# Moving state sums, spread decays, weight loads and weight sums in a fused state-space scan and routed expert layer

## The chip, the cores and the metric

The kernel runs on one core of a Trainium2 chip. Its time is the device time of one execution in microseconds; before the change it was 281.32 us (median of 3 runs, 279.15 to 281.43). The profile is one more execution, recorded on its own: its span, from the first to the last instruction, is 264.6 us. In what follows PE is the matrix engine, DVE the vector engine, ACT the scalar engine, POOL the GpSimd engine and SP the engine that only starts transfers.

## What is computed

The first half is a scan over a state. Batch 4, 8 heads, 768 steps, head size 32, state size 16. Per head, with `a` the decay of each step:

```python
log_a = np.log(np.clip(a, 1e-06, 1.0))
for c in range(nc):                       # chunks of the sequence
    cum = np.cumsum(la, axis=-1)
    L = np.exp(cum[:, :, :, None] - cum[:, :, None, :]) * causal
    M = np.einsum('bhin,bhjn->bhij', Cc, Bc) * L
    y_intra = np.einsum('bhij,bhjd->bhid', M, xc)
    y_inter = np.einsum('bhin,bhnd->bhid', Cc, state) * np.exp(cum)[:, :, :, None]
    y[:, :, sl] = y_intra + y_inter
    state = decay_full[:, :, None, None] * state + np.sum(Bx, axis=2)
```

The second half takes the 3072 tokens of the result, each 256 wide (8 heads of 32), and sends each to one of 8 experts: the one whose embedding has the largest cosine with it. The expert computes `relu(x @ w1[e]) @ w2[e]` with 1024 hidden units, and the result is multiplied by the token's softmax probability for that expert (temperature 0.1), the gate.

## The kernel before

**The scan** works on chunks of 128 steps (6 of them) and on pairs of batches: 12 pairs `p`, two to a chunk. In place of the exponentials of differences it scales: F holds running products of the decays and r their inverses; C is multiplied by F and x by r (x'), and only the causal mask is then left to apply. The steps of one pair, each a function of that name:

- `spread_f` (PE, L278): copies F of the pair's heads over the 16 state rows of each, into PSUM. `scale_c` (DVE, then ACT, L289): C times that, the tile `cp`, and from it two masked copies, `cm`.
- `scale_x` (DVE or POOL, L260): x' for the pair.
- `sums` (PE, L300): B times x' for each batch of the pair. After the second pair of a chunk `states` (DVE, L313) adds them to the decayed old state, the tile `V`, and `next_states` (POOL, L324) decays it into `old`.
- `inner` (PE, L333): B times C for the 8 heads of both batches, into the four PSUM banks of `pg`. `keep_inner` (DVE, L348): that times the mask, two instructions, the tiles `g`.
- `outputs_before` and `outputs_within` (PE, L365 and L381): the part of y from the old state and the part from within the chunk, both summed in PSUM, half of the heads in `pf` and half in `py`. `keep_outputs` (ACT, L396) copies both halves to `yT`.
- `finish` (PE, L412): turns `yT` back to one token to a partition, and computes the 8 routing scores by the same product, into `pz`. `keep_tokens` (ACT, L423) copies this to `yt`.

The main loop of `mamba` (L491) is a software pipeline written out by hand. In its turn `i` it makes F, `cp` and `sums` of pair `i + 2`, `inner` and `g` of pair `i`, outputs of pair `i - 1` and tokens of pair `i - 2`. Below it also routes: `pick` (DVE, even turns) finds each token's expert, `locate` (PE, then DVE, odd turns) its row in that expert's list, and `scatter` (POOL) writes the rows to memory, one transfer for each batch. When four chunks are scattered, the first 208 rows of expert 0 are loaded back as the tile `xe`, and the kernel starts on them (`early`) after the last pair.

The order in this text is the order on every engine: within `manual_schedule` nothing is reordered, and each engine takes its instructions one after the other. Waits between engines are set automatically. In PSUM they are set by whole banks, so that two engines that touch different columns of one bank are put in the order of the text all the same.

**PSUM in the scan** has eight banks: four for `pg`, one for `py`, one for `pf`, two for `pz`. Before the change, `sums` lie in the first 256 columns of `pf` (of `py` for the first chunk), the outputs in the first 256 of `py` and the last 256 of `pf`, the turned outputs in the first 264 of each bank of `pz`, and the spread F beside them, in columns 264 to 391. `locate`, `count` and the turned inverse decays use what is left of `py`.

**The weights** are 2 MB for an expert. `weights` (L239) cuts them in eight transfers of 256 KB: four for `w1` (64 partitions each, rows of 4 KB) and four for `w2` (128 partitions, rows of 1 KB). The loop starts one such transfer a turn from turn 4, three from turn 8; SP waits for nothing in between, so the profile shows 13 of them between 31.7 and 47.2 us.

**The experts.** A job is a set of rows of one expert: `parts[0]` and `parts[1]` are early and late rows of expert 0 (plain products, class `Job`), `parts[2]` and those after it are the whole experts 1 to 7 (class `Seven`, which replaces eight block products by seven and needs sums of weight blocks for it). `mix_up` and `mix_down` (L912, L916) compute these sums on POOL, m1 from `w1` and m2 from `w2`, four instructions each (L909). `mix_x` (DVE, L921) computes differences of the rows, the tile `dx`; `mix_h` (DVE, L989) those of the hidden units. `measure` and `prepare` (L778, L803) compute the gates. `part(i)` (L1072) runs one job; after its gates POOL executes a small copy, the tick (L1123), and then the sums of the job after next. Before the change, m2 of `parts[2]` is computed in the middle of `part(1)`, after the fourth of its eight `up` steps.

Of the kernel before, what the change touches and what calls it, by code (L numbers as in the profile page):

```python
# [226 lines left out]
    k.ld[c] = t  # L227


def load_w1(k, t, w1):  # L230
# [8 lines left out]
def weights(k, e):  # L239

    k.w1t[e] = k.wp.tile([128, KD, F], F32, name="w1", tag="w1")
    yield from load_w1(k, k.w1t[e], k.w1[e])
    k.w2t[e] = k.wp.tile([128, KF, DM], F32, name="w2", tag="w2")
    w2 = k.w2[e].rearrange("(f p) m -> p f m", p=128)
    for f in range(0, KF, 2):
        k.nc.sync.dma_start(k.w2t[e][:, f : f + 2, :], w2[:, f : f + 2, :])
        yield


def load_weights(k, e):  # L250
    for _ in weights(k, e):
        pass


def pair(k, p):
# [16 lines left out]

def forms(k, p):

    return k.pf[:, 0:256].rearrange("p (i m) -> p i m", i=2) if p in (1, 3) else k.pz[:, :, 264:392]


def spread_f(k, p):  # L278
# [21 lines left out]
def sums(k, p):  # L300

    c, b, t = pair(k, p)
    for i in range(2):
        for q in range(4):
            k.nc.tensor.matmul(
                (k.pf if c else k.py)[32 * q : 32 * q + 32, 64 * (b + i) : 64 * (b + i) + 64],
                lhsT=t.b[:, b + i, 32 * q : 32 * q + 32],
                rhs=k.un[p].x[:, i, :].rearrange("p (t q d) -> p q t d", t=2, q=4)[:, q],
                start=True, stop=True, tile_position=(0, 32 * q),
            )  # L310


def states(k, c):  # L313

    nc = k.nc
    st = (k.pf if c else k.py)[:, 0:256].rearrange("p (b m) -> p b m", b=NB)
    V = k.V[c] = k.stp.tile([128, NB, 64], F32, name="V", tag="V")
    if c == 0:
        nc.vector.tensor_copy(out=V[:], in_=st)
        return  # L320
    nc.vector.tensor_tensor(out=V[:], in0=k.old[c - 1][:], in1=st, op=ALU.add)


def next_states(k, c):  # L324
# [71 lines left out]
def keep_outputs(k, p):  # L396
    s = k.un[p]
    s.yT = k.yT[p] = k.work.tile([128, 2, 2, Q], F32, name="yT", tag="yT", bufs=3)
    if p == NU // 2 - 1:
        k.nc.scalar.copy(out=s.yT[:].rearrange("p j i m -> p j (i m)"), in_=k.pg[:, 0:2, 0:256])  # L400
        return
    for j in (1, 0):
        k.nc.scalar.copy(
            out=s.yT[:, j].rearrange("p i m -> p (i m)"), in_=k.pf[:, 256:512] if j == 0 else k.py[:, 0:256]
        )


# [22 lines left out]
def mamba(k):  # L430
# [49 lines left out]
    join(k, 0, k.pz[:, 1, 448:480])  # L480
    keep_inner(k, 1, 1)
    next_states(k, 0)
    outputs_within(k, 0)
    turn_emb(k)
    keep_outputs(k, 0)
    states(k, 1)
    scale_x(k, 4)
    route_consts(k)
    first = (None for e in range(2) for _ in weights(k, e))

    for i in range(2, NP):  # L491
        new = i + 2 if i + 2 < NP else None
# [24 lines left out]
        if pick_now == EC - 1:  # L517
            locate(k, pick_now)
            count_early(k)
        for j in range(2):  # L520
            keep_inner(k, i, j)
        if i < 6:
            next(k.dec[1])
        if pick_now == EC - 1:
            split_early(k)
            scatter(k, pick_now, 0, NB, None)
            load_early(k)
        if i % 2 == 0 and i // 2 < NC - 1:
# [529 lines left out]
def moe(k):  # L1058
# [13 lines left out]
    def part(i):  # L1072
# [14 lines left out]
        if isinstance(j, Seven):  # L1087
            portions = j.measures()
            for f in range(KF // 2):
                if i == EE + 1:  # L1090
                    j.up(f)
                    out(f)
                else:
                    j.up(f, lambda: (out(f), new or next(portions)))
                if not new and f == KF // 2 - 1:

                    k.nc.gpsimd.drain()  # L1097
            j.up(KF // 2, new.turn_x if new else None)
            if not new:
                j.mix_h((1, 0))  # L1100
                j.down_last(lambda: j.prepare(has))
                return
            j.mix_h()
            turn()
            j.down(lambda: j.prepare(has), (lambda: leftover(k)) if i == n - 3 else None)
        else:
            for f in range(KF):
                j.up(f)
                out(f - 1)
                if f == 3:  # L1110
# [214 lines left out]
```

## Time and profile before

| what | value |
|---|---|
| time, median of 3 | 281.32 us |
| span of the profiled execution | 264.6 us |
| scan, from the first `inner` to the last `finish` | 8.3 to 75.9 us |
| load of `xe` started, first use of it | 72.9, 76.2 us |
| first instruction of the first whole expert on PE | 103.2 us |
| time of one turn of the loop (turns 2 to 9, start to start on PE) | 4.5, 4.6, 4.8, 6.0, 8.5, 5.9, 4.5, 5.2 us |
| one `keep_inner` pair, one `scale_c`, one `scale_x` on DVE | 2.35, 0.41, 0.68 us |
| one weight sum on POOL | 1.27 us |

The page lists for each engine its busy time, then 40 equal slices of the span with the busy share of each engine in tenths, the clock that PE was granted in tenths and the share of the DMA engines. A list of waits names who waited for whom, the total, how often, and the longest. A timeline gives start and busy time of each instruction, with the idle time before it and what ended it in brackets.

### The profile page before, as it was taken

The numbers are of one execution on the slowest core, as the hardware profiler recorded it, in microseconds if no ns is written. First come the engines' busy times: TensorE is split into PE (matmuls) and PEld (weight loads), VectorE is DVE, ScalarE is ACT, GpSimd is POOL, SyncE is SP. The second block draws the span as 40 slices with busy tenths as digits, with TensorE's granted clock in tenths as the row PEclk, the third lists the DMA queues.
The fourth block names the chain that finished last, engine by engine and source line by source line (L and its number), as shares of the span: only waits on it lengthen the run. The fifth ranks groups of instructions, "written<-read, shape, count | busy, mean of one in ns | idle before, by whom it ended". The sixth has DMA issues, their size and how long they took to land. (4 is left out here: it accounts for less than half of the span.)

```text
span 264.6 us, 5990 instructions
## 1 busy us (share of the span) xinstructions
PE 244.8 (93%) x2133; PEld 223.4 (84%) x2133; DVE 186.1 (70%) x537; ACT 100.7 (38%) x313; POOL 167.8 (63%) x237
## 2 busy tenths in 40 slices
PE   2999987898989997999999999999999999999990
PEld 1887766776779797899999999999999999999980
DVE  6767897388838449668659668758867866975950
ACT  2335433343344240352445344353355234426310
POOL 4437227275658297992897698498499679635114
PEclk9999999799999999999999999999999999999998
DMA  5989999931262799706708526543570120102002
GB/s 173 385 347 325 383 264 228 233 118 66 108 217 108 164 251 216 210 14 178 221 8 211 176 56 161 150 135 114 120 217 19 44 73 0 55 2 64 0 0 64
DMA packets 19748, 38.89 MB, mean 147 GB/s; under 512 B 2893, under 2 KB 11290, under 8 KB 19717
## 3 DMA queue, kind: packets, MB, share of 16 engines
q1 hardware_dynamic: 16853, 31.94, 43.2%
q0 software_dynamic: 2688, 6.50, 7.8%
q8 instruction: 17, 0.28, 0.5%
q14 instruction: 14, 0.11, 0.2%
q10 hardware_dynamic: 176, 0.06, 0.1%
HBM read 28.37 MB, written 10.37 MB: 146 GB/s over the span
## 5 line engine op out<-in xcount | busy, mean ns | idle before, releaser
L888 POOL DMA_INDIRECT out_dram<-yo,to x32 | 39.5, 1235 | 19.0 <-DVE yo L884 6.3
L932 PE MATMUL sum<-dx,m 128*128 128x208 f32 x168 | 41.1, 349 | 1.8 <-ACT yoT L872 1.5
L940 DVE TENSOR_TENSOR part<-sum,part 128x208 f32<-128x208 f32 x69 | 25.5, 370 | 24.3 <-ACT part L945 17.9
L688 POOL DMA_INDIRECT rows<-yt,row_of x24 | 23.7, 988 | 21.9 <-DVE row_of L677 8.3
L909 POOL TENSOR_TENSOR m<-w 128x512 f32<-128x512 f32 x28 | 35.8, 1278 | 0.2
L940 DVE TENSOR_TENSOR h<-sum,part 128x208 f32<-128x208 f32 x84 | 29.2, 369 | 8.2 <-PE sum L932 5.2
L932 PEld LDWEIGHTS sum<-dx,m 128*128 128x128 f32 x168 | 29.0, 190 | 5.3 <-DVE part L940 3.3
L932 PE MATMUL sum<-dh,m 128*128 128x208 f32 x168 | 30.8, 339 | 0.0
L351 DVE TENSOR_TENSOR g<-pg,mask 128x1024 f32<-128x1024 f32 x24 | 28.3, 1216 | 2.4 <-PE pg L342 2.4
L932 PEld LDWEIGHTS sum<-dh,m 128*128 128x128 f32 x168 | 29.7, 190 | 0.0
L932 PE MATMUL sum<-xT,w 128*128 128x208 f32 x112 | 25.6, 339 | 0.0
L945 ACT COPY part<-sum 128x208 f32<-128x208 f32 x42 | 13.9, 331 | 25.6 <-PE sum L932 25.6
L932 PE MATMUL sum<-h,w 128*128 128x208 f32 x112 | 20.8, 339 | 0.0
L932 PEld LDWEIGHTS sum<-xT,w 128*128 128x128 f32 x112 | 20.1, 190 | 0.0
L985 ACT ACTIVATE h<-h 128x208 f32<-128x208 f32 x28 | 10.6, 377 | 25.1 <-DVE h L940 25.1
L932 PEld LDWEIGHTS sum<-h,w 128*128 128x128 f32 x112 | 19.8, 190 | 0.0
L342 PE MATMUL pg<-cm,bt 32*128 32x256 f32 x192 | 18.4, 463 | 0.8 <-DVE g L351 0.7
L909 POOL TENSOR_TENSOR m<-m,w 128x512 f32<-128x512 f32 x14 | 17.9, 1275 | 1.1
L909 POOL TENSOR_TENSOR m<-w,m 128x512 f32<-128x512 f32 x14 | 18.0, 1284 | 0.0
L800 POOL TENSOR_TENSOR gr<-gr,half 104x4 f32<-104x4 f32 (+1 forms) x9 | 9.2, 1021 | 13.3 <-ACT sq L794 13.3
L976 ACT ACTIVATE h<-h 128x208 f32<-128x208 f32 x28 | 10.6, 377 | 14.2 <-DVE h L940 14.2
L297 ACT ACTIVATE cm<-cp,tmask 128x256 f32<-128x256 f32 x24 | 10.8, 500 | 12.5 <-DVE cp L294 10.6
(234 smaller groups left out, 516.0 us busy)
## 6 DMA issues: line engine op xcount, KB each, us to landing
w<-in_moe_w_dram SPq DMA_DIRECT2D x64, 256.0 KB
rows<-none SPq DMA_DIRECT2D x8, 442.0 KB
xg<-rows SPq DMA_DIRECT2D x7, 442.0 KB
x<-in_x_dram SPq DMA_DIRECT2D x6, 512.0 KB
ct<-in_CT_dram SPq DMA_DIRECT2D x6, 256.0 KB
bt<-in_BT_dram SPq DMA_DIRECT2D x6, 256.0 KB
b<-in_B_dram SPq DMA_DIRECT2D x6, 256.0 KB
out_dram<-yo,to POOLq DMA_INDIRECT x32, 2.6
```

Source lines behind the costliest of these rows:

```text
L297: k.nc.scalar.activation(s.cm[:, :, v, :], s.cp[:], ACT.Copy, scale=k.tmask[:, v : v + 1])
L342: nc.tensor.matmul(k.pg[:, q, 256 * i : 256 * i + 256], lhsT=t.bt[r, b + i, :], rhs=s.cm[r, i], start=True, stop=True, tile_position=(32 * ...
L351: k.nc.vector.tensor_tensor(out=g[:], in0=k.pg[:, :, 256 * i : 256 * i + 256].rearrange("p q (t i) -> p q t i", t=2), in1=k.mask[:].unsque ...
L688: d = nc.gpsimd.indirect_dma_start(out=k.rows[:, :], out_offset=bass.IndirectOffsetOnAxis(ap=k.to[g][:, u : u + 1], axis=0), in_=k.yt[:, N ...
L800: nc.gpsimd.tensor_tensor(out=s.r[:], in0=s.r[:], in1=k.half[0:tr, 0:nt], op=ALU.pow)
L888: d = nc.gpsimd.indirect_dma_start(out=k.out[:, :], out_offset=bass.IndirectOffsetOnAxis(ap=s.to[:, i : i + 1], axis=0), in_=y[:], in_offs ...
L909: s.k.nc.gpsimd.tensor_tensor(out=out, in0=in0, in1=in1, op=op)
L932: s.k.nc.tensor.matmul(ps, lhsT=lhsT(i, g), rhs=rhs(j, g), start=(first and g == gs[0]), stop=(g == gs[-1]), skip_group_check=True,)
L940: s.k.nc.vector.tensor_tensor(out=out, in0=in0, in1=in1, op=ALU.add)
L945: s.k.nc.scalar.copy(out=out, in_=ps)
L976: nc.scalar.activation(o[:, 3], o[:, 3], ACT.Relu)
L985: nc.scalar.activation(o[:, 2], o[:, 2], ACT.Relu)
```

## The change

Four things are moved; what is computed stays the same.

1. `sums` go to columns 264 to 391 of `pz`, beside the turned outputs. They are now issued ahead of `finish`, and `states` follows directly after `keep_tokens`, where it stood after `keep_outputs`. The purpose is that `V` no longer shares a bank with the outputs.
2. The spread F goes to the last 256 columns of `pf`, where `sums` and the second half of the bank made room (in the start-up, for p = 1 to `pz` and for p = 3 to `py`). Both output halves now lie in the first 256 columns. `inner` is issued ahead of `spread_f`. `between` of the start-up moves from `pz` to `py`, and `turn_decays` of the second half of the decays from the middle of turn 5 to its end.
3. The first weights are loaded in the order w2 of expert 0, w1 of expert 0, w1 of expert 1, w2 of expert 1.
4. m2 of the first whole expert is computed after the tick of `part(1)`.

```diff
-    return k.pf[:, 0:256].rearrange("p (i m) -> p i m", i=2) if p in (1, 3) else k.pz[:, :, 264:392]
+    if p == 1:
+        return k.pz[:, :, 264:392]
+    return (k.py[:, 0:256] if p == 3 else k.pf[:, 256:512]).rearrange("p (i m) -> p i m", i=2)
...
-                (k.pf if c else k.py)[32 * q : 32 * q + 32, 64 * (b + i) : 64 * (b + i) + 64],
+                k.pz[32 * q : 32 * q + 32, b // 2, 264 + 64 * i : 328 + 64 * i],
...
-    st = (k.pf if c else k.py)[:, 0:256].rearrange("p (b m) -> p b m", b=NB)
+    st = k.pz[:, :, 264:392]
...
-    return k.pf[:, 256 + 128 * i : 384 + 128 * i] if j == 0 else k.py[:, 128 * i : 128 * i + 128]
+    return (k.py if j else k.pf)[:, 128 * i : 128 * i + 128]
...
-    between(k, 0, k.pz[:, 1, 448:480])
+    between(k, 0, k.py[:, 256:288])
...
     next_states(k, 0)
+    states(k, 1)
     outputs_within(k, 0)
     turn_emb(k)
     keep_outputs(k, 0)
-    states(k, 1)
...
-    first = (None for e in range(2) for _ in weights(k, e))
+    first = (
+        None for p in (w2_portions(k, 0), w1_portions(k, 0), w1_portions(k, 1), w2_portions(k, 1)) for _ in p
+    )
...
+        inner(k, i)
         if new is not None:
             spread_f(k, new)
             scale_c(k, new)
-        inner(k, i)
         if place_now is not None:
             locate(k, place_now)
-        if i == 5:
-            turn_decays(k, 1, k.py[:, 384:512])
...
+        if new is not None and c < NC - 1:
+            sums(k, new)
         finish(k, done)
         keep_tokens(k, done)
+        if new is not None and i % 2 and c < NC - 1:
+            states(k, c)
...
-        if new is not None and c < NC - 1:
-            sums(k, new)
         outputs_before(k, out)
         outputs_within(k, out)
         keep_outputs(k, out)
-        if new is not None and i % 2 and c < NC - 1:
-            states(k, c)
+        if i == 5:
+            turn_decays(k, 1, k.py[:, 384:512])
...
                 if f == 3:
                     j.measure()
-                    parts[EE + 1][0].mix_down()
...
         k.nc.gpsimd.tensor_copy(out=k.tick[:], in_=j.gate[0:1, 0:1])
+        if i == EE:
+            parts[i + 1][0].mix_down()
         if i + 2 < n:
             parts[i + 2][0].mix_up()
             parts[i + 2][0].mix_down()
```

More of the change, by code (lines that the diff above doesn't have):

```diff
@@ L227, in load, with w1_portions @@
     k.ld[c] = t
+def w1_portions(k, e):
+    k.w1t[e] = k.wp.tile([128, KD, F], F32, name="w1", tag="w1")
+    yield from load_w1(k, k.w1t[e], k.w1[e])
 def load_w1(k, t, w1):
@@ L236, in load_w1, with w2_portions @@
             yield
-def weights(k, e):
-    k.w1t[e] = k.wp.tile([128, KD, F], F32, name="w1", tag="w1")
-    yield from load_w1(k, k.w1t[e], k.w1[e])
+def w2_portions(k, e):
     k.w2t[e] = k.wp.tile([128, KF, DM], F32, name="w2", tag="w2")
@@ L250, in load_weights @@
 def load_weights(k, e):
-    for _ in weights(k, e):
-        pass
+    for p in (w1_portions(k, e), w2_portions(k, e)):
+        for _ in p:
+            pass
 def pair(k, p):
@@ L315, in states @@
     nc = k.nc
-    st = (k.pf if c else k.py)[:, 0:256].rearrange("p (b m) -> p b m", b=NB)
+    st = k.pz[:, :, 264:392]
     V = k.V[c] = k.stp.tile([128, NB, 64], F32, name="V", tag="V")
+    v = V[:].rearrange("p (j b) m -> p j (b m)", j=2)
     if c == 0:
-        nc.vector.tensor_copy(out=V[:], in_=st)
+        nc.vector.tensor_copy(out=v, in_=st)
         return
-    nc.vector.tensor_tensor(out=V[:], in0=k.old[c - 1][:], in1=st, op=ALU.add)
+    nc.vector.tensor_tensor(
+        out=v, in0=k.old[c - 1][:].rearrange("p (j b) m -> p j (b m)", j=2), in1=st, op=ALU.add
+    )
 def next_states(k, c):
@@ L403, in keep_outputs @@
         k.nc.scalar.copy(
-            out=s.yT[:, j].rearrange("p i m -> p (i m)"), in_=k.pf[:, 256:512] if j == 0 else k.py[:, 0:256]
+            out=s.yT[:, j].rearrange("p i m -> p (i m)"), in_=(k.py if j else k.pf)[:, 0:256]
         )
@@ L479, in mamba @@
     keep_inner(k, 1, 0)
-    join(k, 0, k.pz[:, 1, 448:480])
+    join(k, 0, k.py[:, 256:288])
     keep_inner(k, 1, 1)
     next_states(k, 0)
+    states(k, 1)
     outputs_within(k, 0)
@@ L485, in mamba @@
     keep_outputs(k, 0)
-    states(k, 1)
     scale_x(k, 4)
     route_consts(k)
-    first = (None for e in range(2) for _ in weights(k, e))
+    first = (
+        None for p in (w2_portions(k, 0), w1_portions(k, 0), w1_portions(k, 1), w2_portions(k, 1)) for _ in p
+    )
     for i in range(2, NP):
```

## The prediction

> **What bounds the kernel now.** I read the page first: the busy lines, the 40 slices and the tables of DMA and waits.
>
> ```profile
> span 264.6 us, 5990 instructions
> PE 244.8 (93%) x2133; PEld 223.4 (84%) x2133; DVE 186.1 (70%) x537; ACT 100.7 (38%) x313; POOL 167.8 (63%) x237
> PE   2999987898989997999999999999999999999990
> PEclk9999999799999999999999999999999999999998
> DMA  5989999931262799706708526543570120102002
> ```
>
> A slice is 6.6 us; I count from 0. From slice 17 (112 us) to about 250 us TensorE (PE) has no gap, so whatever delays the start of that stretch delays the end by as much; what happens inside it on other engines is free. The change therefore pays only through the first 112 us. There slices 5 to 7 (33 to 53 us) show holes and the only low clock before the end, with the DMA engines full until slice 7; slice 15 (99 to 106 us) shows another hole.
>
> The list of waits sizes them: total us, times, longest, over the whole run. Below it the row of PE's timeline (start, busy us) that follows the second wait:
>
> ```profile
> DVE V L321 <- ACT yT L403: 5.1, 4, 2.3
> ...
> PE pf L390 <- issue: 2.2, 1, 2.2
> ```
>
> ```profile
> 47.02 0.43 PE L390 MATMUL pf<-g,xs 128*32 128x128 f32 x3 [2.20 <-issue]
> ```
>
> VectorE (DVE) waits 5.1 us in `states` for ScalarE (ACT) copies of other columns of the same PSUM bank. PE's 2.2 us is no data wait. In the trace, 16 KB packets of instructions come every 250 or so PE records (at records 278, 495, 850, 1209, 1356, 1498); the third and fourth are late, the fourth runs from 44.3 to 45.5 us, and PE stops in the middle of `outputs_within` at 44.5 and goes on at 47.0. I read this as PE out of instructions behind a full DMA queue. The clock is then half from 47.0 to 50.5 us.
>
> The rhythm of the scan stage is in VectorE's timeline, here pairs 8 and 9:
>
> ```profile
> 51.60 2.35 DVE L351 TENSOR_TENSOR g<-pg,mask 128x1024 f32<-128x1024 f32 x2
> 54.77 0.42 DVE L321 TENSOR_TENSOR V<-old,pf 128x256 f32<-128x256 f32 x1 [0.82 <-ACT yT L403]
> 55.11 0.41 DVE L294 TENSOR_TENSOR cp<-ct,pz 128x256 f32<-128x256 f32 x1
> ...
> 56.79 2.34 DVE L351 TENSOR_TENSOR g<-pg,mask 128x1024 f32<-128x1024 f32 x2
> 59.05 0.68 DVE L266 TENSOR_TENSOR xs<-x,rT 128x512 f32<-128x512 f32 x1
> 59.65 0.41 DVE L294 TENSOR_TENSOR cp<-ct,pz 128x256 f32<-128x256 f32 x1
> 60.66 0.19 DVE L673 TENSOR_TENSOR oh<-py,ob 128x32 f32<-128x32 f32 x1 [0.59 <-PE py L668]
> ```
>
> Last, the second hole, on VectorE and on PE:
>
> ```profile
> 97.89 2.85 DVE L928 TENSOR_TENSOR dx<-xT 128x208 f32<-128x208 f32 x2 [0.52 <-ACT xT L836]
> 100.67 2.79 DVE L928 TENSOR_TENSOR dx<-xT,dx 128x208 f32<-128x208 f32 x2
> ...
> 103.51 1.10 DVE L809 COPY_PREDICATED to_f<-late_has,xg 104x2 f32<-104x2 int32 x1
> ```
>
> ```profile
> 105.91 0.59 PE L932 MATMUL sum<-dx,m 128*128 128x208 f32 x2 [1.53 <-ACT yoT L872]
> ```
>
> The four `dx` rows usually take 0.37 us each (the median of that line), here 5.6 us together, while GpSimd (POOL) computes m2. The gates come late behind them, ACT waits 7.1 us for the gates' exponential, so its copy of `yoT` is late, so PE stands 1.5 us for the sum tile that this copy frees.
>
> **What the skill says.** The Trainium skill, "PSUM — Partial Sum Buffer", section "PSUM bank collisions raise a hardware error": engines must be kept apart by bank, not by address; the 5.1 us between a VectorE and a ScalarE read of disjoint columns agrees. "SBUF — State Buffer", section "Who interferes with whom": a VectorE instruction with two SBUF inputs contends with a GpSimd one that reads SBUF, and the loser blocks for the whole instruction; `dx` at up to 2.1 us against 0.37 agrees. Same page, "Door 1: The DMA port swizzle": 64 partitions reach half the ports, 196 GB/s against 328; the trace agrees, 4 KB packets of `w1` (64 partitions) take about 320 ns between 36 and 42 us where those of x (128 partitions) take 159. "TensorE: Matmul & The Clock Gate", Part 1: an idle window of 3.4 us halves the clock; here 2.2 us of standing was followed by 3.4 us at half.
>
> **The change part by part.**
>
> *m2 of the first whole expert behind the gates.* Four POOL rows of 1.27 us move from 99.25 us to after the tick. The four `dx` fall from 5.6 to 1.5 us (up to 2.3 if the 0.85 us power row at 98.4 is met), gates are ready near 102 instead of 106.2, and the 1.53 us of PE go. Behind the tick POOL now has 12 such rows, 15.3 us, to about 117.3 (before: 8 rows to 116.5). The moved m2 is read by the third product of the next `down`, near 120; m1 of the expert after that near 125; the two output scatters queued behind go out 1 us later and nobody waits for them. The last row may meet `mix_h`, which has 5.6 us of products ahead of its first reader. Worth 1.6 us (1.3 to 1.9).
>
> *`states` early, reading pz.* It now stands behind `keep_tokens` (ACT done about 1.3 us before VectorE's `g` ends) and no longer behind `keep_outputs`. The 0.8 to 1.1 us waits of pairs 3, 5 and 7 go. That of 2.3 us at 18.5 us goes too but hid nothing: PE runs on `outputs_within` there.
>
> *`spread_f` in pf, behind `inner`.* Its bank is now freed by ACT's second output copy, about 0.9 us after `outputs_within` ends; `inner` (1.08 us) covers this. But VectorE's queue holds `cp` ahead of `pick` and `g`, and `cp` now needs `inner` and then `spread_f` (0.42 us). From the end of one `g` to the start of the next: 1.5 us of PE, 0.06, then `cp` 0.33, so 1.9 us; `pick` adds 1.35 in even pairs, `locate` 0.6 in odd ones; `g` itself 2.26. That is 5.5 us even and 4.8 us odd. Before, from the rows above: 5.2 (51.60 to 56.79) and 4.4 (56.79 to 61.18). So pairs 8 and 9 get 0.7 us slower: what `states` gives back, `cp` takes. In pairs 2 to 4, where PE sets the pace (4.66 us: 1.5 + 1.1 + 0.36 + 0.6 + 1.0), the same chain adds 0.1 to 0.2 us a pair.
>
> *`sums` ahead of `finish`.* It needs x'; POOL delivers x'(5) at 25.9 and x'(6) at 30.85 (behind its DMA), so PE stands 0.5 and 0.4 us that `finish` used to cover. PE is then 0.4 us late for `inner` of pair 4.
>
> *`turn_decays` at the end of pair 5.* It drops the 0.47 us that PE waited for VectorE's `oh`, but now waits for ACT's copy of the same bank: `inner` of pair 6 starts near 40.2 instead of 39.8.
>
> Following pair by pair: `g`(4) starts at 32.4 (32.1 before), `g`(5) at 37.2 (36.6), `g`(6) at 44.4 (43.7). PE reaches the stop of 44.5 us near 45.2, 0.7 later. What follows depends on the instruction packet. If it is no longer late: `g`(7) starts at 49.3 and the row numbers of chunk 2 are ready at 59.6 instead of 61.27, 1.7 us ahead. If it lands as before (PE on at 47.0): `inner`(7) at 47.9 instead of 46.7; without the low clock 0.5 us ahead, with it 0.8 us behind. From the row numbers on, POOL's eight scatters (61.55 to 71.45, 1.28 us each) and the load of `xe` set the start of the first expert, 14.9 us later (76.17); PE arrives at the same moment (75.9). So this shift reaches the end whole, and gains in pairs 10 and 11 do not.
>
> *Second-layer weights first.* The bytes are the same. Until 54 us nobody reads them. The 1 KB rows of 128 partitions go ahead, the slow `w1` rows are moved together behind them; whether the instruction packet[...] fares better is the unknown. Bounds: from 0 (no pause) to the 2.5 us of before.
>
> *Bank moves at the start* (p = 0 to 3, `between` in py): each has a reader that is done 0.5 us or more before the next writer (for instance `cp` of p = 0 at 7.2 us, `spread_f`(2) at 10.2). No cost.
>
> **How the numbers follow.**
>
> A, likeliest, 0.50: the pause shrinks, since PE comes 0.7 us later and its `inner`(7) would wait for `g`(6) anyway, and the clock stays up. Scan 0.5 to 1.7 ahead, take 1.1; with 1.6 from the gates 2.7 us: 281.3 - 2.7 = 278.6.
>
> B, 0.28: the packet is as late and the clock falls again. Scan 0.8 behind, gates 1.6 ahead: 280.5. For it: the same packet, the same bytes, the slow rows now all in the window in which it is asked for.
>
> C, slower than before, 0.14: VectorE's chain costs more than I worked out, or a second packet is late with the `w1` rows in one block. Pairs 4 to 9 with 0.7 us each give 4.2, less 1.6: 283.9. For it: VectorE is 70 to 100% busy in 30 to 70 us. Against: PE is the bound in pairs 2 to 4.
>
> D, 0.08: no pause, and `cp` overlaps better than I assume, so that the whole of the pause and the low clock (3.7 us) is saved: 281.3 - 3.7 - 1.6 = 276.0.
>
> 1% is 2.8 us, that is below 278.5 or above 284.1. Just under half of A is below 278.5, since its span is 278.0 to 279.2 and my pair-by-pair error is over 1 us; with all of D and a tail of B, 0.45 faster. C is half beyond 284.1, with unknown costs 0.13 slower; the rest, 0.42, within. Taking in D, A and B with their errors and the milder half of C, the range is 275.8 to 283.3.
>
> **What would show it.** `V` waiting for no `yT`, directly after `g`; `cp` waiting for PE; the four `dx` rows near 0.37 us and no wait of PE for `yoT` near 103 us; POOL's run of sum rows as one block of twelve. The pause "issue" of PE near 45 us, its length and the clock after it tell A from B. Wrong I would be if chunk 2's row numbers shift by more than 2 us either way, if `dx` stays slow, or if the twelve rows make a later product wait.

## The result and the profile after

The changed kernel takes 283.71 us (median of 4, 283.56 to 283.96); the kernel before, run beside it, 280.85 us (median of 4). The ratio is 1.0113, 95% interval 1.0066 to 1.0160. So it is about 3 us slower, where I forecast 278.6, and 0.4 us above the range. Ratios are as recorded, formed from the executions taken as undisturbed, while the medians count every execution, so the two need not divide out.

The page of the changed kernel:

```profile
span 282.2 us, 5979 instructions
PE 255.2 (90%) x2133; PEld 231.4 (82%) x2133; DVE 182.2 (65%) x537; ACT 100.3 (36%) x313; POOL 168.5 (60%) x237
PE   2997969997698599999899999999999999999990
PEclk9998995799789979999999999999999999999997
DMA  5989999221143379571751652653653130102002
```

A slice is now 7.05 us. Holes and low clock lie in slices 3 to 14 (21 to 106 us), and DMA is no longer full from slice 7 (49 us) on. But the trace I had predicted from has a span of 264.6 us, some 15 us less than the executions timed before. A fair partner is the trace of the unchanged kernel in e8 below: span 277.1 us, 278.85 us as timed (the median of that run is 280.15 us). Nearly all of the 12.5 us between those two traces of one kernel lie ahead of the first whole expert, whose first product on PE starts at 103.2 us in the one and 115.4 us in the other.

**What came as foreseen.** `V` no longer waits for `yT`; it waits once, for `yt`. What took its place is `cp`. From the list of waits of the changed kernel (who, for whom: total us, times, longest):

```profile
DVE cp L299 <- PE pf L288: 6.2, 6, 2.6
...
PE py L140 <- ACT yT L411: 2.1, 1, 2.1
PE py L676 <- ACT yT L411: 2.0, 1, 2.0
...
PE pz L310 <- POOL xs L269: 1.3, 1, 1.3
...
DVE V L327 <- ACT yt L433: 1.2, 1, 1.2
```

At the gates, VectorE's timeline has the four `dx` at 1.8 us together (5.6 before). But it also has a slow `mix_h`:

```profile
116.40 1.06 DVE L938 TENSOR_TENSOR dx<-xT 128x208 f32<-128x208 f32 x2 [0.52 <-ACT xT L846]
117.39 0.77 DVE L938 TENSOR_TENSOR dx<-xT,dx 128x208 f32<-128x208 f32 x2
...
133.77 3.22 DVE L1005 SCALAR_TENSOR_TENSOR dh<-h 128x832 f32<-128x832 f32 x2
```

**What did not.** PE's timeline, the rows with a wait of over 1.3 us between 20 and 145 us (start, busy, what, and in brackets the idle time ahead and what ended it):

```profile
25.29 0.43 PE L310 MATMUL pz<-xs,b 128*32 128x64 f32 x16 [1.34 <-POOL xs L269]
...
42.54 0.35 PE L140 MATMUL py<-ident,r 128*128 128x128 f32 x1 [2.05 <-ACT yT L411]
...
73.61 0.19 PE L676 MATMUL py<-ob,before_b 128*128 128x32 bf16 x1 [2.03 <-ACT yT L411]
...
99.41 0.97 PE L860 MATMUL pf<-xT,w 128*128 128x208 f32 x4 [3.29 <-ACT hT L864]
```

The first is `sums` of pair 5, now ahead of `finish`; the clock is half from 25.6 to 29.1 us behind it. The second is `turn_decays` at its new place, with `inner` of pair 6 behind it; the clock is half from 42.7 to 52.9 us. The third and fourth have counterparts in the kernel before (e8): from `g` of pair 9 to that of pair 10 it takes 7.56 us here and 7.62 us there, and at the fourth place e8 has stops of 1.92 and 1.74 us. Rows of `dh` and `m` that overlap cost PE once more, at 141 us (below).

Where the time went is seen best in the start of `g`, pair by pair (g(3) is that of pair 3; us, from the traces; the last column is the first product of the first expert):

| kernel | g(3) | g(4) | g(5) | g(6) | g(7) | first expert |
|---|---|---|---|---|---|---|
| before (e8) | 23.6 | 30.3 | 35.8 | 43.4 | 48.3 | 82.9 |
| changed | 24.5 | 33.2 | 38.1 | 49.2 | 55.6 | 89.9 |
| changed, turn_decays in the middle (e7) | 27.1 | 32.9 | 38.3 | 46.5 | 52.5 | 88.6 |
| e7 with eight rows at the gates (e15) | 24.5 | 33.2 | 38.2 | 46.6 | 52.6 | 87.1 |
| changed, three moves undone (e12) | 25.8 | 32.8 | 39.1 | 48.6 | 55.7 | 92.5 |

Single traces of one kernel differ by 1 to 3 us here, so the table tells where, and the ratios tell how much. Against e8 the change is 2.9 us behind at pair 4, 2.4 at pair 5, 5.8 at pair 6 and 7.3 at pair 7, and 7.1 us at the first expert: from pair 8 on nothing more is lost.

### The profile page after: what moved, and what is told of

The parts are those of the page before. It is cut to its first block, busy times and chain, and to the rows that moved or that the text cites. A ratio compares the mean times of both kernels' runs of the same rounds, so it can differ in the third digit from the quotient of the medians.

```text
span 282.2 us, 5979 instructions
## 1 busy us (share of the span) xinstructions
PE 255.2 (90%) x2133; PEld 231.4 (82%) x2133; DVE 182.2 (65%) x537; ACT 100.3 (36%) x313; POOL 168.5 (60%) x237
## 5 line engine op out<-in xcount | busy, mean ns | idle before, releaser
L698 POOL DMA_INDIRECT rows<-yt,row_of x24 | 23.6, 984 | 31.4 <-DVE row_of L687 8.6
L950 DVE TENSOR_TENSOR h<-sum,part 128x208 f32<-128x208 f32 x84 | 29.1, 369 | 8.2 <-PE sum L942 5.2
L942 PE MATMUL sum<-xT,w 128*128 128x208 f32 x112 | 25.6, 339 | 0.0
L955 ACT COPY part<-sum 128x208 f32<-128x208 f32 x42 | 13.9, 330 | 28.7 <-PE sum L942 27.0
L350 PE MATMUL pg<-cm,bt 32*128 32x256 f32 x192 | 19.5, 481 | 3.1 <-DVE g L359 2.9
L995 ACT ACTIVATE h<-h 128x208 f32<-128x208 f32 x28 | 10.6, 377 | 25.1 <-DVE h L950 24.5
L919 POOL TENSOR_TENSOR m<-w,m 128x512 f32<-128x512 f32 x14 | 18.6, 1326 | 0.0
L350 PEld LDWEIGHTS pg<-cm,bt 32*128 32x128 f32 x192 | 11.6, 224 | 8.2 <-DVE g L359 4.4
L425 PE MATMUL pz<-turn,yT 128*128 128x136 f32 x88 | 16.1, 336 | 0.3 <-ACT yT L411 0.3
```

The costliest lines, as they stand in the source:

```text
L350: nc.tensor.matmul(k.pg[:, q, 256 * i : 256 * i + 256], lhsT=t.bt[r, b + i, :], rhs=s.cm[r, i], start=True, stop=True, tile_position=(32 * ...
L425: k.nc.tensor.matmul(token_psum(k, p, i)[:, at : at + Y1], lhsT=yT[:, j, i, :], rhs=k.turn[:, j, :], start=(j == 0), stop=(j == 1), skip_g ...
L698: d = nc.gpsimd.indirect_dma_start(out=k.rows[:, :], out_offset=bass.IndirectOffsetOnAxis(ap=k.to[g][:, u : u + 1], axis=0), in_=k.yt[:, N ...
L919: s.k.nc.gpsimd.tensor_tensor(out=out, in0=in0, in1=in1, op=op)
L942: s.k.nc.tensor.matmul(ps, lhsT=lhsT(i, g), rhs=rhs(j, g), start=(first and g == gs[0]), stop=(g == gs[-1]), skip_group_check=True,)
L950: s.k.nc.vector.tensor_tensor(out=out, in0=in0, in1=in1, op=ALU.add)
```

## The experiments

Each ratio is to the kernel before on the same chip. The first four kernels came to a chip on which the kernel before takes 266.9 us; for the others it takes 280.6 us, as in the result.

| run | median time, us | ratio, 95% interval |
|---|---|---|
| e1 before again | 267.62 | 0.9958 (0.9854 to 1.0062) |
| e2 gates move alone | 265.57 | 0.9971 (0.9902 to 1.0039) |
| e3 scan edits alone | 268.90 | 1.0092 (1.0009 to 1.0174) |
| e4 changed, old order of weights | 266.51 | 1.0013 (0.9942 to 1.0084) |
| e5 changed again | 284.43 | 1.0123 (1.0038 to 1.0208) |
| e6 order of weights alone | 280.10 | 0.9995 (0.9959 to 1.0032) |
| e7 changed, turn_decays in the middle | 282.87 | 1.0083 (1.0052 to 1.0113) |
| e8 before again | 280.15 | 0.9976 (0.9950 to 1.0003) |
| e9 changed, sums late | 283.55 | 1.0103 (1.0040 to 1.0167) |
| e10 changed, spread_f first | 286.92 | 1.0201 (1.0133 to 1.0270) |
| e11 before, eight rows at the gates | 278.95 | 0.9937 (0.9911 to 0.9963) |
| e12 changed, three undone | 289.43 | 1.0327 (1.0247 to 1.0406) |
| e13 turn_decays late, alone | 281.84 | 1.0053 (1.0026 to 1.0080) |
| e14 sums early, alone | 281.38 | 1.0024 (0.9984 to 1.0065) |
| e15 changed, decays and gates mended | 281.50 | 1.0057 (1.0029 to 1.0086) |
| e16 e15 with later constants | 282.27 | 1.0034 (1.0005 to 1.0063) |
| e17 e11 with later constants | 279.86 | 0.9952 (0.9923 to 0.9980) |
| e18 gates move alone | 279.47 | 0.9970 (0.9942 to 0.9998) |

The kernel against itself comes out at 0.9976 in e8, and at 0.9958 on the other chip in e1, so a difference of under 0.3% between two runs says nothing here (0.4% for e2 to e4). The executions of e12 spread from 284.85 to 298.35 us; its two fastest, 284.85 and 287.83, lie 2.0% above the median of the kernel before in the mean.

### The same kernel on two chips: e1, e8, e5

The edit is none: e1 and e8 are the kernel before, e5 the changed one.

> The kernel before, unchanged, to have a trace of an ordinary execution: the traced execution of before took 266.4 us, its timed ones 279.2 to 281.4. Every theory expects 279 to 282 us and a ratio of 1.000 within 0.005. If the stalls that cost the changed kernel its time (completions of a TensorE group that reach ScalarE 1.5 to 4 us late, with TensorE's clock at half after them) belong to the change, this trace has at most one of them and about 266 us; if they belong to the kernel on most executions, it has three or four and a span near 279.

> The kernel before, traced on the chip of this group. If the chip is one on which it takes 281 us, the trace shows where 14 us more than in the first trace go: theory 1, late completions of TensorE groups with half clock after them, three or four between 25 and 105 us, at other places than in the changed kernel; rival, a lower clock all through. If it takes 267 us: the same as in the first trace, 264 to 269.

> The changed kernel, beside the kernel before on the same chip. Theory 1 (instructions: with the first-layer weights ahead, TensorE's packet of instructions lands at 53 to 56 us and TensorE stands 1.8 to 3.0 us at its record 1473, as it did in the runs with the old order; with the second-layer weights ahead the queues are empty at about 48 us and the packet lands in time): on a chip where before takes 267 us it takes 264 to 265.5, ratio 0.993, with no pause named issue after 50 us. Rival 2 (the scan chain itself is slower by 0.7 us a pair and the pause is no part of it): 267 to 269 there, ratio 1.005. On a chip where before takes 281 us, both expect 283.7 again.

e1 gave 267.6 us, e8 280.2 us. In e8 PE stops in places where it does not in e1; here with e1's row for the same instructions last, at 79.94 us, in a fence of its own:

```profile
64.47 1.08 PE L342 MATMUL pg<-cm,bt 32*128 32x256 f32 x4 [0.87 <-issue]
...
89.66 1.16 PE L850 MATMUL pz<-xT,w 128*128 128x208 f32 x4 [1.92 <-issue]
92.55 1.76 PE L850 MATMUL pf<-xT,w 128*128 128x208 f32 x4 [1.74 <-ACT hT L854]
```

```profile
79.94 0.87 PE L850 MATMUL pz<-xT,w 128*128 128x208 f32 x4
```

Between 62 and 66 us of e8 the single records go on in bursts, at 63.0, 63.8, 64.5 and 65.9 us, some 0.7 us or twice that apart. DVE and ACT take the same time for each row on both chips. So the time that I had seen lost in the changed kernel at 73 and 99 us belongs to the chip and not to the change: e8 loses as much there. From `g` of pair 9 to that of pair 10 it takes 7.56 us in the changed kernel, 7.62 in e8, and 4.46 in e1. The changed kernel took 1.0123 again in e5. The pause at PE's record 1473, which my theory for e5 was about, showed in e3 and e4 (1.8 and 3.0 us, idle by issue), and on the slower chips in e14 and e17 (1.9 and 0.8 us). These are four of the eleven traces with the old order of the weights, two with the changed scan and two with the scan as before; none of the nine with the new order, e5 among them, has it. That speaks for theory 1, but so few traces do not decide it, and a gain in time does not show (e6, below).

### The gates: e2, e18, e11

e2 and e18 are one kernel: the kernel before with the change's move of `mix_down`. e11 has this instead:

```diff
-                    parts[EE + 1][0].mix_down()
...
+        if EE <= i < n - 1:
+            parts[i + 1][0].mix_down()
         if i + 2 < n:
             parts[i + 2][0].mix_up()
-            parts[i + 2][0].mix_down()
```

> Only the move of the first whole expert's second sums behind the gates. Theory 1 (the move gains 1.5 us at the gates and gives 0.6 back where its last row meets the mix_h row; the scan edits cost the rest): 0.9 us faster, 280.0, ratio 0.997. Rival 2 (the move gives back more than it gains: POOL's row at 134 us slows mix_h, the output scatters and the second sums of this expert, and TensorE stands 1.7 us and loses clock): 1 to 3 us slower, 282 to 284.

> Only the gates move of the change, with twelve rows behind the first tick, on the chip of this group. Theory 1: 1.0 us faster, ratio 0.9965 (0.7 us less gain than the eight rows, which had 0.9937). Rival (the twelfth row costs nothing and the two are the same): 0.9937.

> The kernel before with the second sums of every expert but the next behind the tick, so that POOL has 8 rows behind each gate and none of them meets mix_h. Theory 1 (the move of the change gains 1.5 us at the gates, and loses 0.6 to 1.3 where its twelfth row meets mix_h): 1.4 us faster than before, ratio 0.995, VectorE's two rows of dh at 1.95 us together and no wait of TensorE for part in the first whole expert's down. Rival (the loss at the down comes from the late output scatters): a wait of 0.6 us or more stays, ratio 0.997.

The move alone has 0.9971 on one chip and 0.9970 on the other, 0.8 us of 280.6, each at the edge of what a run can tell; with eight rows behind each tick it is 0.9937, 1.8 us. In the changed kernel, POOL's twelve rows run to 136.1 us. The last of them, with the output transfer behind it, on POOL:

```profile
134.06 2.04 POOL L919 TENSOR_TENSOR m<-w,m 128x512 f32<-128x512 f32 x1
...
136.34 1.59 POOL L898 DMA_INDIRECT out_dram<-yo,to  x1 [0.20 <-issue]
```

It meets `mix_h`, which takes 3.22 us for two instructions. The first reader of `dh` does not wait, which I had foreseen; but PE waits for `part`, which stands behind `mix_h` in DVE's queue (in the same kernel):

```profile
141.26 1.67 PE L942 MATMUL sum<-dh,w 128*128 128x208 f32 x8 [0.97 <-DVE part L950]
```

In e11 the same `mix_h` meets nothing. From its start to that of the row `part` that PE waited for it takes 5.81 us instead of 7.07, and no wait of PE is left in that `down`:

```profile
131.43 1.96 DVE L995 SCALAR_TENSOR_TENSOR dh<-h 128x832 f32<-128x832 f32 x2
```

The Trainium skill, "SBUF — State Buffer", section "Who interferes with whom", says that the loser of such a meeting is blocked for the whole instruction. The single records agree, and each side loses once: POOL's row starts at 134.06 us behind DVE's first row of `dh` (133.77 to 134.98 us) and takes 0.77 us more than alone, and DVE's second row starts at 134.90 us behind POOL's and takes 2.08 us, 1.06 more than in e11. e11 also moves m2 of the later experts; that the whole difference between e11 and e18 comes from this one meeting was not tested apart, but it has the size of the 0.97 us that PE stands.

### The order of the weights: e4, e6

```diff
-        None for p in (w2_portions(k, 0), w1_portions(k, 0), w1_portions(k, 1), w2_portions(k, 1)) for _ in p
+        None for p in (w1_portions(k, 0), w2_portions(k, 0), w1_portions(k, 1), w2_portions(k, 1)) for _ in p
```

That is e4; e6 puts the new order into the kernel before.

> The changed kernel with the first expert's first-layer weights loaded first again. Theory 1: the order of the weights is worth nothing, 283.7 within 0.7. Rival 3 (with the second-layer weights first the slow half-width packets of the first layer lie where TensorE's instructions are fetched, which makes the late stalls): about before minus 1, 280.

> The kernel before with the order of the weights alone changed. Theory 1: the pause of 1.3 to 2.2 us at TensorE's record 1217 (44.5 to 47.9 us) is not touched[...] or shrinks by up to 1.5 us as the queues drain earlier: ratio 0.994 to 1.000. Rival 2 (order worth nothing): 1.000 with the queues full as long as before.

e6 has 0.9995: the order is worth nothing that can be told. Its pause at record 1217 is 1.64 us, no smaller than the 0.74 us of e8. e4 came to the chip with 266.9 us; its ratio, 1.0013, is lower than the 1.0113 of the changed kernel, but the intervals overlap (and e3, which has the same scan, has 1.0092). The changed kernel itself was not run on that chip.

### All scan edits together: e3

It has the changed kernel's scan, the old order of weights and the old place of `mix_down`.

> Only the scan edits (places in PSUM, spread_f behind inner, sums and states early, turn_decays late), with the weights in the old order and the second sums in the old place. Theory 1 (the scan edits are what costs): 3 to 4 us slower, 284 to 285. Rival 2 (the gates move costs): within 1 us of before. Rival 3 (the order of the weights costs): within 1 us of before.

0.9% or 2.5 us slower (the times in the expectations of e2 to e4 assume a kernel before of 281 us, so the ratios are to be read). Theory 1 had 3 to 4 us; the interval holds both that and almost nothing. Its trace is on the same chip as e1, so the two can be laid side by side. Pair 4 on DVE in e1, then in e3:

```profile
28.13 0.42 DVE L321 TENSOR_TENSOR V<-old,pf 128x256 f32<-128x256 f32 x1 [1.67 <-ACT yT L403]
28.96 0.42 DVE L294 TENSOR_TENSOR cp<-ct,pz 128x256 f32<-128x256 f32 x1 [0.41 <-DMA ct<-in_CT_dram]
...
30.55 2.35 DVE L351 TENSOR_TENSOR g<-pg,mask 128x1024 f32<-128x1024 f32 x2
```

```profile
28.78 0.42 DVE L327 TENSOR_TENSOR V<-old,pz 128x256 f32<-128x256 f32 x1 [1.41 <-ACT yt L433]
31.57 0.42 DVE L299 TENSOR_TENSOR cp<-ct,pf 128x256 f32<-128x256 f32 x1 [2.37 <-PE pf L288]
...
33.17 2.35 DVE L359 TENSOR_TENSOR g<-pg,mask 128x1024 f32<-128x1024 f32 x2
```

The 1.67 us of `V` shrink by 0.26 us only, since DVE now waits for `yt`, which PE delivers late. Then `cp` waits 2.37 us for `spread_f`, and with it everything of pair 4 is 2.6 us later. Not all of this is due to the queue: ahead of it PE stands 1.37 us for x' of pair 5 and runs at half clock from 25.3 to 28.7 us, which e1 does not. In e1 PE makes up `sums` of pair 6 late (1.85 us for B), so that by `g` of pair 5 the two are level, 38.26 and 38.12 us; in e8 that wait is 0.89 us and the lead stays.

### turn_decays: e7, e13

e7 is the changed kernel with this, e13 the kernel before with the reverse:

```diff
         if place_now is not None:
             locate(k, place_now)
+        if i == 5:
+            turn_decays(k, 1, k.py[:, 384:512])
...
         keep_outputs(k, out)
-        if i == 5:
-            turn_decays(k, 1, k.py[:, 384:512])
```

> The changed kernel with turn_decays back in the middle of turn 5, ahead of the outputs. Theory 1 (its new wait for ScalarE's copy costs TensorE 0.5 us at 40 us, or 2 us where TensorE's completion comes late, ahead of inner of pair 6): 0.5 us faster than the changed kernel where before takes 267 us, 2 to 4 us where before takes 281. Rival: VectorE's chain sets pair 6 anyway and the move is worth nothing, within 0.3 us of the changed kernel.

> The kernel before with turn_decays alone moved to the end of pair 5. Theory 1 (there it waits for ScalarE's copy of the second half of the outputs, with inner of pair 6 behind it): TensorE stands 0.5 to 2.4 us near 40 us at the line of turn_decays, and the whole is 1 to 2 us slower than before (ratio 1.004 to 1.007). Rival (it costs only together with the new places, by the low clock after it): within 0.5 us of before.

e13 settles it: this one move makes the kernel before 1.5 us slower (1.0053), with the wait foreseen by theory 1:

```profile
41.03 0.33 PE L140 MATMUL py<-ident,r 128*128 128x128 f32 x1 [1.63 <-ACT yT L403]
```

Here `turn_decays` writes the bank that `keep_outputs` has just begun to read. ACT's copy waits for PE's outputs to end and be told of; `inner` of pair 6 stands behind `turn_decays`, so PE is idle for the whole round trip. From `g` of pair 5 to that of pair 6 it takes 9.1 us in e13, 7.7 us in e8, 11.1 us in the changed kernel and 8.2 us in e7. By the ratios e7 gains 0.4% back (1.0083 against the 1.0123 of e5), 1.1 us, less than theory 1 had for this chip.

### Orders and places: e9, e10, e12, e14

```diff
# e9, and e14 the other way round in the kernel before (without states)
-        if new is not None and c < NC - 1:
-            sums(k, new)
         finish(k, done)
         keep_tokens(k, done)
...
+        if new is not None and c < NC - 1:
+            sums(k, new)
         outputs_before(k, out)
# e10
-        inner(k, i)
         if new is not None:
             spread_f(k, new)
             scale_c(k, new)
+        inner(k, i)
```

e9 moves `states` along with `sums`. e12 has e7, e9 and e10 together.

> The changed kernel with sums and states put back behind finish, keep_tokens and the scatters of the turn; their place in pz is kept. Theory 1 (ahead of finish TensorE stands 1.6 us at 23.7 us for x' of pair 5 and its clock then halves for 3.4 us; in the runs without that, it stands for B or x' of pair 6): g of pair 4 starts 1.5 to 2.5 us earlier and the whole is 1.5 to 2 us faster than the changed kernel (ratio to before about 1.005 where the changed kernel has 1.012). Rival (POOL and VectorE set pair 4 anyway): within 0.5 us of the changed kernel, and the wait for x' is found in front of another line.

> The changed kernel with spread_f and scale_c ahead of inner again. Theory 1 (behind inner, VectorE's cp waits for TensorE's spread_f, 0.5 us in each odd turn): the turns 5, 7 and 9 shorten by 0.3 to 0.5 us each, 1 to 1.5 us faster than the changed kernel. Rival: spread_f then stands in front of inner for ScalarE's copy of the same bank, inner is late by as much, and nothing or up to 2 us is lost.

> The changed kernel with three undone together: sums and states late, spread_f first, turn_decays in the middle. What is left are the places in PSUM, the weights' order and the gates move. Theory 1 (these three are the whole loss of the scan, the places cost nothing): 0.9 us faster than before, ratio 0.997. Rival (the places themselves cost, for one pz is now shared by finish, the sums and their readers): 1.003 to 1.012, with waits of TensorE for ScalarE's yt copy in front of the sums.

> The kernel before with sums alone put ahead of finish. Theory 1 (the wait for x' of pair 5 is no longer covered by finish, TensorE stands 1.6 us near 24 us and its clock halves): g of pair 4 starts 1 to 2.5 us later, the whole 0.5 to 2 us slower (ratio 1.002 to 1.007). Rival (the wait only moves, for B and x' of pair 6 come late in either order and pair 5 begins when it did): within 0.5 us.

Here my theory fell. I took the new orders for the loss; undone one by one, `sums` and `spread_f` gain nothing (e9, 1.0103 against 1.0123) or lose (e10, 1.0201), and undone together with `turn_decays` they lose at least as much: e12 has 1.0327, or 1.020 by its two fastest executions, where e7, with `turn_decays` alone undone, has 1.0083. In e12 PE waits for ACT's `yT` in every turn and for its `yt` in turns 3, 5 and 7. Two turns of it:

```profile
36.75 0.37 PE L288 MATMUL pf<-f,spread 32*128 32x128 f32 x1 [0.82 <-ACT yT L411]
...
40.76 0.43 PE L310 MATMUL pz<-xs,b 128*32 128x64 f32 x16 [0.69 <-ACT yt L433]
...
44.41 0.59 PE L288 MATMUL pf<-f,spread 32*128 32x128 f32 x3 [0.79 <-ACT yT L411]
```

`spread_f` now lies in the bank that ACT copies to `yT`, `sums` in the banks that ACT copies to `yt`. So it is the places that cost, and the orders of the change hide a good part of that cost: `inner` covers the wait for `yT`, `finish` comes after `sums`. The prediction had this right for `spread_f` (freed 0.9 us late, covered by `inner`). e14, with the order of `sums` alone in the old places, has 1.0024, which decides nothing.

### What is left: e15, e16, e17

e15 is e7 with the gates of e11. e16 and e17 add this to e15 and e11:

```diff
-    route_consts(k)
...
             scale_x(k, new + 1)
+        if i == 2:
+            route_consts(k)
```

> The changed kernel with turn_decays in the middle of pair 5 and eight rows behind each gate. Theory 1 (both parts add up): 1.6 us faster than the changed kernel by the first, 0.8 by the second, so 0.4 to 0.5 per cent slower than before (ratio 1.003 to 1.006); what is left is the start of pair 4, about 2 us later than before. Rival (the rows at the gates do not add, since the first expert then waits elsewhere): 1.008 as with the first part alone.

> The changed kernel with turn_decays in the middle, eight rows behind each gate, and POOL's constants for the router computed after x' of pair 5 instead of before it. Theory 1 (the remaining loss comes from TensorE's wait for x' of pair 5 ahead of finish and the half clock after it): no wait at 23.6 us, full clock until 40 us, g of pair 4 at 30.5 to 31.5 instead of 33.2 us, and the whole 2 to 2.5 us faster than with the two mended parts alone, ratio to before 0.997 to 0.999. Rival 2 (spread_f behind inner and VectorE's cp behind it set pair 4): the wait goes, but g of pair 4 starts no more than 0.7 us earlier, ratio 1.003 to 1.006.

> The kernel before with eight rows behind each gate and the same later constants. Theory 1: its wait of 0.9 us for x' of pair 5 goes, but B and x' of pair 6 come late anyway, so it is within 0.5 us of the eight rows alone, ratio 0.992 to 0.995. Rival: 0.9 us more, ratio 0.990.

e15 has 1.0057, as the sum of the two parts says. Against the kernel before with the same gates (e11, on another chip) 1.2% is left: 1.0057 / 0.9937 = 1.0121, 3.4 us. e16 and e17, run together on one chip, differ by the scan and the order of the weights alone: 1.0034 / 0.9952 = 1.0082, 2.3 us. e16 has 1.0034, which is rival 2's number: the wait for x' of pair 5 is worth some 0.6 us, and even that is within the 0.3% that says nothing. (Its trace doesn't show that edit at work: there the first `g` is 1.3 us late, because the transfer of `bt` (B turned) came late, and the second row of `g` of pair 1 starts another 0.7 us later than in e15; a trace with that later start, e5, has no such wait without the edit either.) e17 is no faster than e11: in the kernel before, the wait for x' is not on the path.

The traces of e16, e18, e7 and e17 start alike (from the first `g` to its second row of pair 1 it takes 6.74 to 6.76 us), so they show where the rest lies. From that row, and then from `g` of one pair to that of the next, in us:

| to pair | 2 | 3 | 4 | 5 | 6 | 7 | 8 | 9 | 10 |
|---|---|---|---|---|---|---|---|---|---|
| e18 (scan as before) | 4.21 | 4.18 | 6.08 | 4.51 | 7.81 | 4.86 | 6.63 | 4.91 | 7.64 |
| e17 (scan as before, later constants) | 4.13 | 4.19 | 6.70 | 4.51 | 7.91 | 5.74 | 6.77 | 6.51 | 7.62 |
| e16 (changed scan, turn_decays and constants mended) | 4.94 | 4.55 | 5.87 | 4.96 | 8.37 | 6.00 | 6.56 | 4.94 | 7.68 |
| e7 (changed scan, turn_decays mended) | 4.95 | 4.55 | 5.78 | 5.36 | 8.24 | 6.04 | 6.53 | 4.94 | 7.67 |

Against e18, e16 loses 0.4 to 0.7 us in each of pairs 2, 3, 5 and 6, 1.1 us in pair 7, and gains 0.2 in pair 4: 3.0 us in all, and nothing from pair 8 on. This may be too much, since the traced execution of e16 took 2.2 us more than the median of its run and that of e18 2.4 us less; from e17 to e16 it is 1.5 us, from e18 to e7 3.3 us. Steady over these four traces are the 0.4 us of pair 3 and 0.4 us or more of pair 5. Pair 7 is not: the scan as before has 4.86 us without the pause at record 1217, but 5.74 and 6.92 us with one of 1.6 and 2.8 us (e17, e11), and e16 and e7 have half clock just ahead of it (46.1 to 49.5 and 45.1 to 48.6 us), where e8, e11, e17 and e18 have full clock all through these pairs. How much of the loss is the clock's was not separated.

Pairs 2 to 7 are the turns that still make `sums` of a later pair. What DVE waits for in them is `cp`. Pair 3 in e18, then in e16, DVE and below it PE:

```profile
24.96 0.39 DVE L294 TENSOR_TENSOR cp<-ct,pz 128x256 f32<-128x256 f32 x1
25.67 2.36 DVE L351 TENSOR_TENSOR g<-pg,mask 128x1024 f32<-128x1024 f32 x2 [0.33 <-PE pg L342]
```

```profile
27.64 0.42 DVE L299 TENSOR_TENSOR cp<-ct,pf 128x256 f32<-128x256 f32 x1 [0.72 <-PE pf L288]
28.09 2.36 DVE L359 TENSOR_TENSOR g<-pg,mask 128x1024 f32<-128x1024 f32 x2
```

```profile
25.95 1.15 PE L350 MATMUL pg<-cm,bt 32*128 32x256 f32 x16 [0.34 <-DVE g L359]
26.93 0.60 PE L288 MATMUL pf<-f,spread 32*128 32x128 f32 x4
```

In the kernel before, `spread_f` is ahead of `inner`, in a bank whose reader is long done, and `cp` can be computed while `inner` runs. Behind `inner`, `cp` comes after both, and `g`, whose products are there at 27.1 us, comes after `cp`. In pair 8 the same chain costs nothing, for there it takes the place of `V`'s wait: `V` waits 2.25 us in e18 and `cp` none, in e16 `V` none and `cp` 2.30 us.

e11 is the fastest of all, 1.8 us faster than before: the change's fourth part, with one more edit.

## Why the prediction was wrong

The forecast was a sum of two gains, 1.1 us from the scan and 1.6 us from the gates. The gates gave 0.8 us (e18). The scan is the term that failed, in sign: it cost about 4 us (the 3.2 us measured and the 0.8 us of the gates; e3 alone has 2.5 us). Against the starts that I had followed pair by pair, `g`(4) 32.4, `g`(5) 37.2, `g`(6) 44.4 and `g`(7) 49.3, the trace has 33.2, 38.1, 49.2 and 55.6: the largest break is ahead of pair 6, at `turn_decays`, though by e7 only 1.1 us of it reaches the end.

**The partner.** I worked from one trace with a span of 264.6 us and subtracted from a time of 281.3 us; its 266.4 us as timed is what the chip of e1 gives, though on which chip it was taken is not on record. The pause of 2.2 us at 44.5 us, on which case A rests with 1.1 us, comes and goes: at the same record (1217) PE is idle by issue in eight of the eleven traces with the old order of the weights (0.5 us in e4 to 2.8 us in e11, not at all in e1 and e18) and in one of the nine with the new order (1.6 us in e6). In the changed kernel it is gone, which was my sign of A, but no gain in time shows for it. The half clock does not belong to it: it followed the pause in the trace before and in e6, and not in e2, e3, e8, e11, e14 and e17. The term "weights first, 0 to 2.5 us" measured 0, with an interval of 1 us either way (e6).

**The gates, 1.6 us: the gain was right in mechanism, half in size.** `dx` fell to 1.8 us and PE's wait for `yoT` went. The term that failed is "the last row may meet `mix_h`, which has 5.6 us of products ahead of its first reader", costed at nothing. It did meet it, and the sign that I had named for being wrong, a later product that waits for the twelve rows, came. I had looked at the reader of `dh` only; `mix_h` took 1.3 us more, the row `part` behind it on DVE came late by as much, and PE stood 1.0 us for it. The two output transfers behind the last row took 1.6 and 1.7 us on POOL instead of 1.0. Of 1.8 us (e11) 0.8 us were left (e18).

**turn_decays, 0.4 us: the step was mis-sized.** "Now waits for ACT's copy of the same bank: `inner` of pair 6 starts near 40.2 instead of 39.8." The wait was named; that nothing of PE lies ahead to fill it, and that ACT's copy itself can't start until PE's own completion is seen, was not. The wait measured 2.05 us, with a half clock behind it, in the changed kernel; the move cost 1.5 us of time alone (e13) and 1.1 us there (e7).

**cp behind inner and spread_f, 0.1 to 0.2 us in pairs 2 to 4 and 0.7 us later: the mechanism was right, the pairs were the wrong ones, and it stood in the wrong case.** I made PE the bound in pairs 2 to 4 and DVE after them, up to pair 9 (the sum in brackets for PE's pace makes 4.56 us, not 4.66). My chain gave 0.3 us for an even and 0.4 us for an odd pair, 0.7 us for pairs 8 and 9 together. Pairs 3 and 5 lose just that, 0.4 us each, and all the pairs with `sums`, 2 to 7, lose 0.25 to 0.55 us each in the mean (1.5 to 3.3 us in all); pairs 8 and 9 lose nothing on this chip, where pair 9 takes 4.91 us even in e18, against 4.39 in e1. In A I let the pause of before pay for that. C, with 4.2 us for it and 283.9 us in all, has the measured time, in part by luck: its "pairs 4 to 9 with 0.7 us each" is this mechanism, but 0.7 us is what I had worked out for two pairs, and part of what it stood for was really `turn_decays`.

**sums ahead of finish, 0.5 us:** PE was idle 1.3 us at x' of pair 5 in the profiled execution, because it came 1.4 us earlier than I had it and x' only 0.6. It is no steady cost: a trace with a later start, e5, has no such wait, and taking it away gave some 0.6 us (e16).

**What `states` gives back:** the 5.1 us of `V` were to pay for `cp`. I had seen for the first of these waits that its end gains nothing; no run shows a gain from the end of the others, and in pair 8 `cp` takes just what `V` gives back, as I had written.

The sum: gates -0.8 (e18), turn_decays +1.5 (e13), the rest of the scan +2.3 (e16 over e17) to +3.4 (e15 over e11), weights 0, together +3.0 to +4.1, where 3.2 us (1.0113 of 280.85 us) and 3.5 us (e5) were measured; each term has an error of about 0.8 us. This rest is the new places and the orders that these force; that is what remains, not what a run with the places alone showed. How the rest divides between `spread_f` behind `inner` and `sums` ahead of `finish` was not separated, since `sums`, spread F and outputs change places together.

## What to carry to other kernels

A wait on an engine that has slack is no gain to be had: before a tile is moved to another bank to end it, list who reads the new bank, and which engine then stands. A transpose or product that writes a bank just handed to a copy can cost its whole round trip if the engine's next work stands behind it. And when a row is moved behind others on a slow engine, the last row of the new block is what has to be timed, against everything behind the row that it meets; splitting the block in equal parts (8 and 8 rows for 12 and 8) kept the whole gain here.

## What the runs showed of the hardware

- One kernel takes 266.9 us on one chip and 280.6 us on two others, with the same duration of the DVE and ACT rows compared. The difference lies before the first whole expert: on the slower chips PE stops in steps of about 0.7 us, or its completion is seen late (PE's waits for `hT` of 1.7 us in e8, 3.3 us in the changed kernel and 4.0 us in e11), and its clock falls for it (mean 0.990 in e1, 0.971 in e8). The stops that I looked at closely (62 to 66 and 87 to 92 us in e8) lie while POOL starts its indirect transfers of token rows; on the other chip the same transfers run without them. The cause was not found, and no run here leaves the transfers out.
- A pause of 1.3 to 1.4 us (to 25.3 us) was enough to halve PE's clock for 3.4 us in the changed kernel and in e3, e15, while a pause of 2.8 us in e11 (44.3 to 47.0 us) left it full until 66 us. So the length of a single pause did not decide. The Trainium skill, "TensorE: Matmul & The Clock Gate", Part 1, gives an idle window of 3.4 us; the length of the low clock agrees (3.41 us, or two or three times that), but the pause ahead of it was shorter.
